# Retention attention and a feed-forward on one core: the lead-in's order of work, V scaled ahead of the masks, transposes two units ahead, all tables first

## The chip, the cores and the metric

The kernel runs on one core of one Trainium2 chip. The time is device microseconds of one execution of the whole program, loads and stores of HBM included; below, "time" is the median of several executions, and "span" the part of the one profiled execution between its first and last instruction. Engines: PE does matmuls (PEld its weight loads), DVE and ACT elementwise work, POOL (GpSimd) issues the loads, SP the stores and the DMA transposes.

## The reference

For 8 batches and 8 heads of 576 positions with head size 64, retention attention (no softmax, a decay by distance), and then a feed-forward layer on the 4608 tokens:

```python
scores = (q @ k.transpose(0, 1, 3, 2)) / sqrt(64)
gamma = 1 - 2 ** (-5 - arange(H))
ret = scores * where(rel >= 0, gamma ** rel, 0)      # rel = query position - key position
x = (ret @ v).transpose(0, 2, 1, 3).reshape(4608, 512)
h = x @ w_in                                         # 512 -> 2048
out = (h * sigmoid(1.702 * h)) @ w_out               # 2048 -> 512
```

All inputs and the output are float32 in HBM.

## The kernel before, in words

**Units and chunks.** The 4608 tokens are cut into 36 units of 128 rows; four units make a chunk of 512 tokens, so there are 9 chunks. Each pair of batches gives nine units: four of the first batch, four of the second, and one that joins the last 64 rows of both. The decay factors out as gamma^i * gamma^-j: V is scaled by gamma^-j (table `vfac`), the output by gamma^i (table `gq`), and in between only a 0/1 mask is needed. Earlier units of the same batch come in through a state, the sum of K^T V so far.

**The steps of one unit u**, by the names of the helpers:

- `transpose_pe(u, bank, eng)`: eight 128 x 128 transposes of K and Q on PE into a PSUM bank (L310), then one copy to SBUF, tile `qkT`, on ACT (L314) or DVE (L317). From unit 12 on the transposes are done by DMA from SP's queue instead (L322).
- `scores(u, 0)`: eight matmuls into banks S0 and S1 (L398); `scores_out(u, hh, 0)`: two DVE multiplies by the mask, tiles `pm_0` and `pm_1` (L407).
- `scale_v(u)`: one DVE multiply of V by `vfac`, tile `vp` (L301).
- `state_in_psum(u, "S3", eng)` or, from unit 8, `state(u, "S3")`: four matmuls of K by `vp` (L331), then copies into tile `kv` (ACT L344, DVE L346; for `state` four DVE operations from L359 on). A unit that joins two batches has none.
- `inter(u)`: matmuls of the state up to the unit before (L379, L386), none for the first unit of a batch; `values(u)`: eight matmuls of `vp` by the masked scores (L417); `values_out(u)`: one DVE multiply by `gq` into the chunk's `xT` (L427).

The feed-forward of a chunk is 16 steps `up` (four matmuls of 512 columns, L438, and a gelu on ACT, L443) and 16 steps `down` (four matmuls, L469; every fourth ends a unit: copy on ACT, L477, and store by SP, L483). Chunk 1's ups are done in halves of 256 tokens, `up_half` (L455, L460).

**The order.** Each engine works its own queue strictly in the order in which the code lists its operations; semaphore waits are derived from the tiles and PSUM banks read and written. The order of the first twelve units ("heads") is written out by hand: a lead-in with units 0 to 3, the ups of chunks 0 and 1 with units 4 to 7 between, and the downs of chunk 0 with units 8 to 11 between. `play(n, step, events)` runs n steps and calls the listed events after the step of that number. From unit 12 on (the "blocks", two units each) a loop repeats one pattern. `warm(n)` puts n matmuls of a zero tile into PE's queue (L491); their output is not used.

**Loads.** POOL issues K and Q of a unit (`load_kq`), V (`load_v`) and the weights in one queue: units 0 to 3, w_in, units 4 to 7, w_out, units 8 and on. V of units 0 and 1 alone comes over SP's queue at the very start. A load waits only until its buffer is free (12 buffers of K and Q, 10 of V).

**Tables.** `setup_first`, `setup_gq` and `setup_last` make masks and tables on DVE and ACT; `setup_last` has the parts that the joined units need. `setup_gelu` loads ACT's function table for gelu, `setup_tail` makes the joined units' mask and clears the second batch's state tiles.

Of the kernel before, what the change touches and what calls it, by code (L numbers as in the profile page):

```python
# [140 lines left out]
def bass_retnet_parallel__then__act_gelu_quick_kernel(  # L141
# [13 lines left out]
    with es:  # L155
# [40 lines left out]
        def load_kq(u):  # L196
            sl = u % NLD
            rows = unit_rows(u)
            for i, src in enumerate((k, q)):
                def f(e, src=src, i=i):  # L200
                    return [
                        e.dma_start(  # L202
                            kq[sl][p0 : p0 + n, i, :].rearrange("p (h d) -> p h d", d=DH),
                            src[b, :, s0 : s0 + n, :].rearrange("h p d -> p h d"),
                        )
                        for p0, n, b, s0 in rows
                    ]
                op("pool", f, writes=[f"kq{sl}_{i}"], dma=f"d_kq{sl}_{i}", ndma=len(rows))
# [51 lines left out]
        def setup_gq(c0, c1):  # L260
            for hp in range(HP):
                op("act", lambda e, hp=hp: e.activation(
                    gq[:, c0:c1, hp, :],
                    iota_c[:, P * c0 : P * c1].rearrange("p (c i) -> p c i", i=P),
                    AF.Exp, bias=lnsc.ap(), scale=lng[:, hp : hp + 1]),
                   reads=["iota_c", "lnsc", f"lng{hp}_0", f"lng{hp}_1"],
                   writes=[f"gq{hp}_{c}" for c in range(c0, c1)])
# [17 lines left out]
        def setup_gelu():  # L285
            op("act", lambda e: e.activation(scr.ap(), lnsc.ap(), AF.Gelu_apprx_sigmoid),
               reads=["lnsc"], writes=["scr"])
# [11 lines left out]
        def scale_v(u):  # L299
            sl, _, ty = u % NVN, *unit_info(u)[1:]  # L300
            op("dve", lambda e: e.tensor_tensor(  # L301
                vp[u % NVP].ap(), vn[sl].ap(),
                vfac[:, ty, :, None].to_broadcast([P, H, DH]), ALU.mult),
               reads=[f"vn{sl}"] + (VF if ty < 4 else VFT), writes=[f"vp{u % NVP}"])
# [65 lines left out]
        def inter(u):  # L370
            pb, kind, c = unit_info(u)
            qt = qkT[u % NQT]
            if c == 0:
                return
            bank = f"O{u % 2}"
            ob = by_pair(bank)
            for hp in range(HP):
                if kind < 2:
                    op("pe", lambda e, hp=hp: e.matmul(  # L379
                        ob[:, hp, :], kv[kind][c - 1][:, hp, :], qt[:, HP + hp, :],  # L380
                        start=(hp == 0), stop=True, skip_group_check=True),
                       reads=[f"kv{kind}_{c - 1}_0", f"kv{kind}_{c - 1}_1", f"qkT{u % NQT}"],
                       writes=[bank])
                else:
                    for b in range(2):
                        op("pe", lambda e, hp=hp, b=b: e.matmul(  # L386
                            ob[:, hp, 64 * b : 64 * b + 64], kv[b][3][:, hp, :],
                            qt[:, HP + hp, 64 * b : 64 * b + 64],
                            start=(hp == 0 and b == 0), stop=True, skip_group_check=True),
                           reads=[f"kv{b}_3_0", f"kv{b}_3_1", f"qkT{u % NQT}"], writes=[bank])  # L390

        def scores(u, sb0=None):
            sb0 = 2 * (u % 2) if sb0 is None else sb0
            qt = qkT[u % NQT]
            for hp in range(HP):
                for hh in range(2):
                    bank = f"S{sb0 + hh}"
                    op("pe", lambda e, hp=hp, hh=hh, bank=bank: e.matmul(  # L398
                        by_pair(bank)[:, hp, :], qt[64 * hh : 64 * hh + 64, hp, :],
                        qt[64 * hh : 64 * hh + 64, HP + hp, :], skip_group_check=True),  # L400
                       reads=[f"qkT{u % NQT}"], writes=[bank])

        def scores_out(u, hh, sb0=None):
            sb0 = 2 * (u % 2) if sb0 is None else sb0
            m = maskc if unit_info(u)[1] == 2 else mask
            bank = f"S{sb0 + hh}"
            op("dve", lambda e: e.tensor_tensor(  # L407
                pm[u % 4][hh].ap(), by_pair(bank), m[:, None, :].to_broadcast([P, HP, P]), ALU.mult),
               reads=[bank, "maskc" if m is maskc else "mask"], writes=[f"pm{u % 4}_{hh}"])

        def values(u):
            c = unit_info(u)[2]
            bank = f"O{u % 2}"
            ob = by_pair(bank)
            for hp in range(HP):
                for hh in range(2):
                    op("pe", lambda e, hp=hp, hh=hh: e.matmul(  # L417
                        ob[64 * hh : 64 * hh + 64, hp, :], vp[u % NVP][:, 2 * hp + hh, :],
                        pm[u % 4][hh][:, hp, :],
                        start=(c == 0 and hp == 0), stop=True, skip_group_check=True),  # L420
                       reads=[f"vp{u % NVP}", f"pm{u % 4}_{hh}"], writes=[bank])

        def values_out(u):
            ch, j = divmod(u, 4)
            ty = unit_info(u)[2]
            bank = f"O{u % 2}"
            op("dve", lambda e: e.tensor_tensor(  # L427
                xT[ch % 3][:, :, 128 * j : 128 * j + 128], by_pair(bank), gq[:, ty, :, :], ALU.mult),
               reads=[bank] + [f"gq{i}_{ty}" for i in range(HP)], writes=[f"xT{ch % 3}_{j}"])
# [58 lines left out]
        def warm(n):  # L488

            for _ in range(n):  # L490
                op("pe", lambda e: e.matmul(  # L491
                    banks["H1"].ap(), zero[:, 0:P], zero.ap(), start=True, stop=True),
                   reads=["zero"], writes=["H1"])

        def head_in(u, eng, bank="S2"):
            transpose_pe(u, bank, eng)

        def head_mid(u, eng):
            scores(u, 0)
            scores_out(u, 0, 0)  # L500
            scores_out(u, 1, 0)
            scale_v(u)
            if u < 8:
                state_in_psum(u, "S3", eng)
            else:
                state(u, "S3")

        def head_out(u):
            inter(u)
            values(u)  # L510
            values_out(u)

        def fetch(m):
            for u in (2 * m, 2 * m + 1):
# [45 lines left out]
        setup_first()  # L560
        setup_gq(0, 1)
        setup_gq(1, 4)
        load_kq(0)
        load_kq(1)
        for u in (2, 3):
# [16 lines left out]
                for f in events.get(i, ()):  # L582
                    f()

        warm(14)
        head_in(0, "dve")
        warm(3)
        head_mid(0, "act")
        warm(1)
        head_in(1, "act")  # L590
        warm(1)
        head_out(0)
        warm(1)
        head_mid(1, "act")
        warm(1)
        head_in(2, "act")
        warm(2)
        head_out(1)
        warm(1)
        head_mid(2, "act")  # L600
        setup_last()
        warm(1)
        head_in(3, "act")
        warm(2)
        head_out(2)
        warm(2)
        head_mid(3, "act")
        setup_gelu()
        setup_tail()
        warm(6)  # L610
        head_out(3)
        for u in (10, 11):
            load_kq(u)
            load_v(u)
        warm(4)
        play(16, lambda f: up(0, f), {
            10: [lambda: head_in(4, "dve")],
            12: [lambda: head_mid(4, "dve")],
            14: [lambda: head_out(4), lambda: head_in(5, "dve")],
        })  # L620
        head_mid(5, "dve")
        head_in(6, "dve")
        warm(4)
        head_out(5)
        fetch(6)
        warm(6)
        play(8, lambda i: up_half(1, i, 0), {
            0: [lambda: head_mid(6, "dve")],
            2: [lambda: head_in(7, "dve"), lambda: head_out(6)],
            4: [lambda: head_mid(7, "dve")],  # L630
            6: [lambda: head_out(7)],
        })
        fetch(7)
        play(8, lambda i: up_half(1, i, 1), {})
        play(16, lambda i: down(0, i, ("S2", "H1")), {
            2: [lambda: head_in(8, "act", "H0")],
            4: [lambda: head_mid(8, "dve")],
            6: [lambda: head_out(8), lambda: head_in(9, "act", "H0")],
            8: [lambda: head_mid(9, "dve")],
            10: [lambda: head_out(9), lambda: head_in(10, "act", "H0"), lambda: ready(6)],  # L640
            12: [lambda: head_mid(10, "dve")],
            13: [lambda: head_in(11, "act", "H0")],
            14: [lambda: head_out(10)],
            15: [lambda: head_mid(11, "dve"), lambda: fetch(8)],
        })
        play(4, lambda i: down(1, i, ("H0",)), {1: [lambda: head_out(11)]})
        for m in range(5, NU // 2 + 1):
# [74 lines left out]
```

## Time and profile before

| | |
|---|---|
| time, three executions | 344.62 us median (342.09 to 344.97) |
| the profiled execution | 346.53 us, of which span 344.7 us |
| mean granted TensorE clock in the profile | 0.965 |
| busy in the span | PE 311.8 us, DVE 131.5, ACT 127.3, POOL 106.7 |
| moved | 39.14 MB at 114 GB/s in the mean |
| first up step of chunk 0 starts at | 35.18 us |
| first down step of chunk 0 starts at | 80.25 us |
| first scores of unit 12 (blocks start) | 111.85 us |

How to read the rows of the profile: a row of the timeline has start and duration in us, engine, source line, operation, output <- inputs, shapes and the number of instructions that were merged, and in brackets how long the engine stood idle before and what released it. A row that lists stretches has the busy time of each engine with the number of instructions. A granted clock of 1.00 is full speed, 0.50 half. A row of DMA issues ends in the time from issue to landing.

### The profile page before, as it was taken

What the parts mean: (1) busy time and instruction counts of PE and PEld (TensorE: products, weight loads), DVE (VectorE), ACT (ScalarE), POOL (GpSimd) and SP (SyncE); (2) the same over time, 40 slices, a digit from 0 to 9 for tenths busy, and PEclk for the clock granted to TensorE, in tenths of its full rate; (3) what the DMA queues carried; (4) which work ended last, traced back from release to release, by engine and by line L of the source; (5) the groups of instructions that cost most, each with busy time, mean ns of one, the idle gap of its engine ahead of it and who ended that gap; (6) DMA issues with size and microseconds to landing.
All of it is one profiled execution on the core that took longest, in us unless ns stands there. A gap on an engine that the chain in (4) does not pass through costs nothing.

```text
span 344.7 us, 5147 instructions
## 1 busy us (share of the span) xinstructions
PE 311.8 (90%) x2157; PEld 161.0 (47%) x2193; DVE 131.5 (38%) x265; ACT 127.3 (37%) x226; POOL 106.7 (31%) x133
## 2 busy tenths in 40 slices
PE   7477977699777999999999999999999999999995
PEld 2343334575333454545545454545455454544442
DVE  3535046620665571705363553507262643100000
ACT  7253541244121433343433334343434333344411
POOL 9999748430525534360515160000000000000000
PEclk9855999999899999999999999999999999999999
DMA  9999999991999999998799999404040411100022
GB/s 134 194 204 178 203 191 177 178 158 28 124 136 133 154 174 154 126 155 137 96 128 155 84 176 127 91 33 91 33 91 32 95 60 25 37 30 30 32 91 61
DMA packets 114712, 39.14 MB, mean 114 GB/s; under 512 B 103809, under 2 KB 107905, under 8 KB 114689
## 3 DMA queue, kind: packets, MB, share of 16 engines
q0 software_dynamic: 82016, 22.55, 64.2%
q1 hardware_dynamic: 32672, 16.26, 26.3%
q8 instruction: 17, 0.28, 0.3%
q14 instruction: 7, 0.05, 0.1%
HBM read 36.70 MB, written 9.44 MB: 134 GB/s over the span
## 4 chain that ended last, share of the span: by engine, by line
PE 84%; DVE 6%; DMA 4%; ACT 2%; issue 2%; POOL 1%; SPq 1%; POOLq 0%; DVEq 0%
PE psS L469 30%; PE psH L438 30%; PE psH L455 4%; PE psS L398 3%; PE psO L417 3%; PE psH L469 3%; DMA qkT<-kq 3%; PE psS L331 3%; PE psH L491 2%; PE psO L469 2%; DVE pm_0 L407 2%; DVE vp L301 2%; DVE pm_1 L407 2%; PE psO L379 2%; DMA kq<-in_q_dram 1%
## 5 line engine op out<-in xcount | busy, mean ns | idle before, releaser
L438 PE MATMUL psH<-xT,w_in_sb 128*128 128x512 bf16 x498 | 125.8, 379 | 1.0 <-ACT osb L477 0.2
L443 ACT ACTIVATE gT<-psH 128x512 bf16<-128x512 f32 x128 | 76.4, 597 | 134.3 <-PE psH L438 134.3
L469 PE MATMUL psS<-w_out_sb,gT 128*128 128x512 bf16 x480 | 122.2, 383 | 2.6 <-DVE pm_0 L407 2.2
L438 PEld LDWEIGHTS psH<-xT,w_in_sb 128*128 128x128 bf16 x512 | 49.0, 98 | 60.8 <-ACT gT L443 3.5
L469 PEld LDWEIGHTS psS<-w_out_sb,gT 128*128 128x128 bf16 x496 | 46.9, 98 | 52.4 <-issue 1.6
L202 POOL DMA_DIRECT2D kq<-in_k_dram x40 | 36.8, 927 | 60.1 <-PE psS L331 57.3
L216 POOL DMA_DIRECT2D vn<-in_v_dram x38 | 35.0, 932 | 38.5 <-DVE vp L301 33.7
L202 POOL DMA_DIRECT2D kq<-in_q_dram x40 | 36.7, 926 | 0.3 <-issue 0.2
L427 DVE TENSOR_TENSOR xT<-psO,gq 128x512 bf16<-128x512 f32 x36 | 23.6, 684 | 26.2 <-PE psO L417 26.2
L331 PE MATMUL psS<-vp,kq 128*128 128x128 bf16 x128 | 13.0, 227 | 21.8 <-DVE vp L301 21.8
L407 DVE TENSOR_TENSOR pm_0<-psS,mask 128x512 bf16<-128x512 f32 x32 | 22.0, 688 | 27.5 <-PE psS L398 27.5
L361 DVE TENSOR_TENSOR kvf<-psS,kvf 64x256 f32<-64x256 f32 x24 | 10.1, 422 | 36.7 <-PE psS L331 36.5
L477 ACT ACTIVATE osb<-psS 128x512 f32<-128x512 f32 x31 | 18.5, 597 | 15.1 <-PE psS L469 15.1
L301 DVE TENSOR_TENSOR vp<-vn,vfac 128x512 bf16<-128x512 f32 x36 | 23.6, 681 | 0.0
L331 PEld LDWEIGHTS psS<-vp,kq 128*128 128x128 bf16 x128 | 9.2, 100 | 28.8 <-DVE vp L301 23.8
L407 DVE TENSOR_TENSOR pm_1<-psS,mask 128x512 bf16<-128x512 f32 x32 | 21.8, 680 | 0.0
L491 PE MATMUL psH<-zero 128*128 128x512 bf16 x46 | 17.2, 500 | 1.5 <-DVE zero L242 1.2
L460 ACT ACTIVATE gT<-psH 128x512 bf16<-128x512 f32 x16 | 9.6, 597 | 17.7 <-PE psH L455 17.7
L455 PE MATMUL psH<-xT,w_in_sb 128*128 128x256 bf16 x128 | 14.8, 273 | 0.0
L359 DVE COPY kvf<-psS 64x256 f32<-64x256 f32 x12 | 5.1, 422 | 24.5 <-PE psS L331 24.4
L398 PE MATMUL psS<-qkT 64*128 64x128 bf16 x288 | 12.9, 224 | 1.1 <-ACT qkT L314 0.7
L417 PE MATMUL psO<-pm_0,vp 128*64 128x128 bf16 x144 | 13.5, 233 | 0.0
(74 smaller groups left out, 183.3 us busy)
## 6 DMA issues: line engine op xcount, KB each, us to landing
out_dram<-osb SPq DMA_DIRECT2D x32, 256.0 KB, 2.3
vn<-in_v_dram POOLq DMA_DIRECT2D x30, 256.0 KB, 10.5
kq<-in_k_dram POOLq DMA_DIRECT2D x32, 128.0 KB, 6.3
kq<-in_q_dram POOLq DMA_DIRECT2D x32, 128.0 KB, 9.1
w_in_sb<-in_moe_w_in_dram POOLq DMA_DIRECT2D x4, 512.0 KB, 9.5
w_out_sb<-in_moe_w_out_dram POOLq DMA_DIRECT2D x4, 512.0 KB, 18.1
vn<-in_v_dram POOLq DMA_DIRECT2D x8, 128.0 KB, 7.5
out_dram<-osb SPq DMA_DIRECT2D x8, 128.0 KB, 2.4
```

The lines of the kernel that those rows point to most:

```text
L202: e.dma_start(kq[sl][p0 : p0 + n, i, :].rearrange("p (h d) -> p h d", d=DH), src[b, :, s0 : s0 + n, :].rearrange("h p d -> p h d"),)
L216: e.dma_start(vn[sl][p0 : p0 + n, :, :], v[b, :, s0 : s0 + n, :].rearrange("h p d -> p h d"),)
L301: op("dve", lambda e: e.tensor_tensor(vp[u % NVP].ap(), vn[sl].ap(), vfac[:, ty, :, None].to_broadcast([P, H, DH]), ALU.mult), reads=[f"vn ...
L331: op("pe", lambda e, hp=hp: e.matmul(kb[:, hp, :], kq[sl][:, 0, P * hp : P * hp + P], vp[u % NVP][:, 2 * hp : 2 * hp + 2, :], start=(first ...
L407: op("dve", lambda e: e.tensor_tensor(pm[u % 4][hh].ap(), by_pair(bank), m[:, None, :].to_broadcast([P, HP, P]), ALU.mult), reads=[bank, " ...
L417: op("pe", lambda e, hp=hp, hh=hh: e.matmul(ob[64 * hh : 64 * hh + 64, hp, :], vp[u % NVP][:, 2 * hp + hh, :], pm[u % 4][hh][:, hp, :], st ...
L427: op("dve", lambda e: e.tensor_tensor(xT[ch % 3][:, :, 128 * j : 128 * j + 128], by_pair(bank), gq[:, ty, :, :], ALU.mult), reads=[bank] + ...
L438: op("pe", lambda e, a=a: e.matmul(hb, w_in_sb[:, a, P * f : P * f + P], xT[c % 3][:, a, :], start=(a == 0), stop=(a == HP - 1)), reads=[f ...
L443: op("act", lambda e: e.activation(gT[c % 2][:, f, :], hb, AF.Gelu_apprx_sigmoid), reads=[bank], writes=[f"gT{c % 2}_{f}"])
L455: op("pe", lambda e, a=a, f=f, j=j: e.matmul(hb[:, j, :], w_in_sb[:, a, P * f : P * f + P], xT[c % 3][:, a, n], start=(a == 0), stop=(a == ...
L469: op("pe", lambda e, f=f: e.matmul(y, gT[c % 2][:, f, P * r : P * r + P], w_out_sb[:, f, :], start=(f == 0), stop=(f == NF - 1)), reads=[f ...
L491: op("pe", lambda e: e.matmul(banks["H1"].ap(), zero[:, 0:P], zero.ap(), start=True, stop=True), reads=["zero"], writes=["H1"])
```

## The change

- `setup_last()` is called with the other tables, ahead of everything else, instead of after unit 2's first half.
- `head_mid` is now scores, scaling of V, masks; the state moves out of it to the end of `head_out`, behind inter, values and `values_out`. The scaling of V for units 0 and 1 is listed ahead of all heads.
- The lead-in's transposes stand further ahead: unit 1's directly behind unit 0's scores, unit 2's ahead of unit 1's scores, unit 3's ahead of unit 2's. They use banks H0 and S2 in turn, where before they all used S2.
- Unit 0's `head_out` comes behind unit 1's `head_mid`, and so on. The numbers of fillers change, 49 to 30 in sum.
- Units 4 to 7 are placed earlier in the ups: unit 5 and unit 6's transposes move into chunk 0's ups.
- In the downs of chunk 0 the places of the events stay, but `head_mid` and `head_out` have their new contents.

```diff
-        def head_mid(u, eng):
+        def head_mid(u):
             scores(u, 0)
+            if u > 1:
+                scale_v(u)
             scores_out(u, 0, 0)
             scores_out(u, 1, 0)
-            scale_v(u)
+
+        def head_out(u, eng="dve"):
+            inter(u)
+            values(u)
+            values_out(u)
             if u < 8:
                 state_in_psum(u, "S3", eng)
             else:
                 state(u, "S3")
-
-        def head_out(u):
-            inter(u)
-            values(u)
-            values_out(u)
...
         setup_gq(1, 4)
+        setup_last()
...
-        warm(14)
+        scale_v(0)
+        scale_v(1)
+        warm(13)
         head_in(0, "dve")
+        warm(4)
+        head_mid(0)
+        head_in(1, "act", "H0")
         warm(3)
-        head_mid(0, "act")
+        head_in(2, "act")
+        head_mid(1)
+        head_out(0, "act")
+        head_in(3, "act", "H0")
         warm(1)
-        head_in(1, "act")
-        warm(1)
-        head_out(0)
-        warm(1)
-        head_mid(1, "act")
-        warm(1)
-        head_in(2, "act")
+        head_mid(2)
+        head_out(1, "act")
         warm(2)
-        head_out(1)
-        warm(1)
-        head_mid(2, "act")
-        setup_last()
-        warm(1)
-        head_in(3, "act")
-        warm(2)
-        head_out(2)
-        warm(2)
-        head_mid(3, "act")
+        head_mid(3)
+        head_out(2, "act")
         setup_gelu()
+        warm(4)
+        head_out(3, "act")
         setup_tail()
-        warm(6)
-        head_out(3)
...
-        warm(4)
+        warm(2)
         play(16, lambda f: up(0, f), {
-            10: [lambda: head_in(4, "dve")],
-            12: [lambda: head_mid(4, "dve")],
-            14: [lambda: head_out(4), lambda: head_in(5, "dve")],
+            9: [lambda: head_in(4, "dve")],
+            11: [lambda: head_mid(4)],
+            12: [lambda: head_in(5, "dve")],
+            13: [lambda: head_out(4)],
+            14: [lambda: head_mid(5)],
+            15: [lambda: head_in(6, "dve"), lambda: head_out(5)],
         })
-        head_mid(5, "dve")
-        head_in(6, "dve")
-        warm(4)
-        head_out(5)
         fetch(6)
-        warm(6)
+        head_mid(6)
+        head_in(7, "dve")
+        warm(1)
         play(8, lambda i: up_half(1, i, 0), {
-            0: [lambda: head_mid(6, "dve")],
-            2: [lambda: head_in(7, "dve"), lambda: head_out(6)],
-            4: [lambda: head_mid(7, "dve")],
-            6: [lambda: head_out(7)],
+            1: [lambda: head_out(6)],
+            3: [lambda: head_mid(7)],
+            5: [lambda: head_out(7)],
         })
```

More of the change, by code (lines that the diff above doesn't have):

```diff
@@ L636, in bass_retnet_parallel__then__act_gelu_quick_kernel @@
             2: [lambda: head_in(8, "act", "H0")],
-            4: [lambda: head_mid(8, "dve")],
+            4: [lambda: head_mid(8)],
             6: [lambda: head_out(8), lambda: head_in(9, "act", "H0")],
-            8: [lambda: head_mid(9, "dve")],
+            8: [lambda: head_mid(9)],
             10: [lambda: head_out(9), lambda: head_in(10, "act", "H0"), lambda: ready(6)],
-            12: [lambda: head_mid(10, "dve")],
+            12: [lambda: head_mid(10)],
             13: [lambda: head_in(11, "act", "H0")],
             14: [lambda: head_out(10)],
-            15: [lambda: head_mid(11, "dve"), lambda: fetch(8)],
+            15: [lambda: head_mid(11), lambda: fetch(8)],
         })
```

## The prediction

> **What bounds the kernel now.** I read the time by stages first. The cuts are where the first up-projection starts (35.18), where the down-projection of chunk 0 starts (80.25) and where the steady blocks start (111.85). The columns are start:end, length, busy time of PE, PEld, DVE, ACT and POOL, granted clock, DMA share and rate.
>
> ```profile
> 0.00:35.18 35.18, 24.06 (x162) 12.55 (x165) 14.66 (x41) 16.05 (x42) 34.55 (x48) 0.71 1.57 178
> 35.18:80.25 45.07, 37.00 (x324) 23.33 (x327) 16.27 (x28) 18.53 (x32) 23.06 (x28) 1.00 1.61 171
> 80.25:111.85 31.60, 25.51 (x200) 12.70 (x203) 16.65 (x30) 6.73 (x9) 12.05 (x14) 0.95 0.86 113
> 111.85:344.73 232.88, 225.25 (x1474) 112.42 (x1500) 83.90 (x166) 85.97 (x144) 37.03 (x45) 1.00 0.68 93
> ```
>
> The last stage, two thirds of the span, has PE busy for 225.25 of 232.88 us; its code is not touched, and I move it as a block. What the change can win lies ahead of 111.85. The same cut for the filler line, and the waits, say how much is loose there (waits from 35.18 to 111.85: total us, times, longest):
>
> ```profile
> 0.00:35.18 35.18, 14.90 (x37) 4.47 (x39) 0.71 1.57 178
> ```
> ```profile
> PE psS L331 <- DVE vp L301: 13.9, 7, 2.0
> ```
>
> Of 24.06 us of PE work in the lead-in, 14.90 is filler. Seven times in the next two stages, once a unit, PE stands 2.0 us at the state matmuls (L331) until V is scaled; the timeline of the lead-in has the same wait at 10.57, and shows why:
>
> ```profile
> 7.45 0.69 DVE L317 COPY qkT<-psS 128x1024 bf16<-128x1024 bf16 x1 [4.06 <-PE psS L310]
> ...
> 8.63 0.69 DVE L407 TENSOR_TENSOR pm_0<-psS,mask 128x512 bf16<-128x512 f32 x1 [0.49 <-PE psS L398]
> ...
> 9.83 0.68 DVE L301 TENSOR_TENSOR vp<-vn,vfac 128x512 bf16<-128x512 f32 x1
> ...
> 10.57 0.51 PE L331 MATMUL psS<-vp,kq 128*128 128x128 bf16 x4 [1.98 <-DVE vp L301]
> ...
> 11.12 0.77 ACT L344 ACTIVATE kv_0<-psS 64x256 bf16<-64x256 f32 x2 [4.29 <-PE psS L331]
> ...
> 12.40 1.02 ACT L314 ACTIVATE qkT<-psS 128x1024 bf16<-128x1024 bf16 x1 [0.51 <-PE psS L310]
> ...
> 13.40 0.69 DVE L427 TENSOR_TENSOR xT<-psO,gq 128x512 bf16<-128x512 f32 x1 [2.88 <-PE psO L417]
> ...
> 23.45 1.65 ACT L271 ACTIVATE gq<-iota_c,lnsc,lng 128x128 f32<-128x128 f32 x4
> ...
> 25.00 0.84 ACT L281 ACTIVATE vfac<-iota_t 128x1 f32<-128x1 f32 x8
> ```
>
> A unit is one chain: transposes, copy, scores, two mask multiplies, scaling of V, state, then the next unit's transposes behind it in PE's queue, 5 to 7 us a unit.
>
> **The change, step by step.** (1) *Tables.* The 1.65 + 0.84 us on ACT leave their place ahead of unit 3's copy. They now follow this row:
>
> ```profile
> 2.81 4.02 ACT L262 ACTIVATE gq<-iota_c,lnsc,lng 128x128 f32<-128x128 f32 x8
> ```
>
> ACT is then free at 6.83 + 2.49 = 9.3. Little is late: unit 1's transposes, the first that ACT copies, follow scores(0), which start at 8.2, by 0.35 + 0.45 and end about 9.0 (prices below); the 0.3 lie under the wait for unit 2's load. Without that cover it would cost 2.5.
>
> (2) *scale_v ahead of the masks.* It runs while PE does scores or ups, so the 2.0 us of each wait goes; the state now follows the values matmuls, which wait for the masks. What is late next is pm_1: two mask multiplies after the scores, 1.3 us by their starts 0.61 apart and 0.68 long. Units 0 and 1 are scaled as soon as V lands, before DVE has anything else. The wait added is DVE's on V's load: the masks are queued behind it, and PE's values behind them.
>
> (3) *Transposes two units ahead.* In PE's queue head_in(2) now stands ahead of scores(1), and head_in(3) ahead of scores(2): PE waits for q of unit 3 with unit 2's scores behind it. The load queue's rows, issue and landing, for q of units 3, 4 and 13, and for w_in (the median of its four):
>
> ```profile
> 8.77 0.96 POOL L202 DMA_DIRECT2D kq<-in_q_dram  x1
> ```
> ```profile
> kq<-in_q_dram POOLq DMA_DIRECT2D x1, 128.0 KB, 5.2
> ```
> ```profile
> 14.33 1.02 POOL L202 DMA_DIRECT2D kq<-in_q_dram  x1
> ```
> ```profile
> kq<-in_q_dram POOLq DMA_DIRECT2D x1, 128.0 KB, 12.7
> ```
> ```profile
> 49.29 0.87 POOL L202 DMA_DIRECT2D kq<-in_q_dram  x1 [0.25 <-issue]
> ```
> ```profile
> kq<-in_q_dram POOLq DMA_DIRECT2D x1, 128.0 KB, 14.8
> ```
>
> ```profile
> 10.52 3.07 POOL L225 DMA_DIRECT2D w_in_sb<-in_moe_w_in_dram  x4
> ```
> ```profile
> w_in_sb<-in_moe_w_in_dram POOLq DMA_DIRECT2D x4, 512.0 KB, 9.5
> ```
>
> The q land at 14.0, 27.0 and 64.1. POOL's queue is not reordered, so I keep these times. PE's prices at full clock come from the up stage, where an up step (four matmuls) follows from the starts of two gelus eight steps apart, (43.80 - 36.89) / 8 = 0.86:
>
> ```profile
> 36.89 0.60 ACT L443 ACTIVATE gT<-psH 128x512 bf16<-128x512 f32 x1 [0.27 <-PE psH L438]
> ...
> 43.80 0.60 ACT L443 ACTIVATE gT<-psH 128x512 bf16<-128x512 f32 x1 [0.27 <-PE psH L438]
> ```
> ```profile
> 51.51 0.62 PE L310 MATMUL psS<-ident,kq 128*128 128x128 bf16 x8
> ...
> 51.96 1.03 PE L438 MATMUL psH<-xT,w_in_sb 128*128 128x512 bf16 x4
> ```
> ```profile
> 56.88 0.39 PE L379 MATMUL psO<-qkT,kv_0 128*128 128x128 bf16 x4
> ...
> 57.20 0.24 PE L417 MATMUL psO<-pm_0,vp 128*64 128x128 bf16 x1
> ...
> 57.55 1.47 PE L491 MATMUL psH<-zero 128*128 128x512 bf16 x6
> ```
>
> By the distance of the starts: head_in 0.45, inter 0.32, values 0.35. Scores (eight small matmuls in pairs, like values) I take as 0.35, state (four, like inter) as 0.32 at most; a filler is a quarter of an up step, 0.22.
>
> *Lead-in.* q of unit 3 lands at 14.0, its transposes leave PE at 14.2; ACT copies until 15.4. Scores(2) 14.4 to 14.75; DVE, which has scaled V of unit 2 by then, masks until 16.1. Inter(1), values(1), state(1), two fillers: to 16.1. Scores(3) 16.2; DVE has xT of unit 1 (0.7), scale_v(3) (0.7) and the masks to do: until 18.6. PE meanwhile does head_out(2), ACT its state and the gelu table; values(3) from 18.7, xT of unit 3 behind xT of unit 2 on DVE: 19.9. So the first up starts at **20.0** instead of 35.18. The weights do not hold it: w_in is issued from 10.5 to 13.6 and takes 9.5, so to about 23, the last quarter being wanted only 12 steps after the first up, at 30.
>
> *Ups of chunks 0 and 1.* 32 steps x 0.86 = 27.6. Heads 4 to 7: 4 x (0.45 + 0.35 + 0.35 + 0.32) + 3 x 0.32 = 6.8, one filler 0.2, and the first values' wait for pm_1 in units 5 and 6, 0.5 + 0.3, as no up stands between. 35.4 us, so down starts at **55.4** instead of 80.25. q of unit 4 is asked for at 20.0 + 10 steps = 28.6 and is there at 27.0.
>
> *Down of chunk 0.* 20 steps, 17.3; heads 8 to 11, where unit 8 has no state and unit 9 no inter, 4 x (0.45 + 0.35 + 0.35) + 6 x 0.32 = 6.5; waits for pm at units 10 and 11, where DVE has just had scaling of 12 and 13 (1.3) and four state pieces (1.75): 0.5 and 1.1. 25.4, so the blocks start at **80.8** instead of 111.85. Here three of the 2.0 us waits go, and a stretch at half clock that they lead to (92.6, below; half of 3.4 us, 1.7).
>
> My placing leaves out small hops. Doing the old 35.18 to 80.25 the same way (27.6 + 6.8, ten fillers 2.2, four waits of 2.0) gives 44.6 for 45.07, the old down stage (17.3 + 6.5, three waits 6.0, clock 1.7) 31.5 for 31.60: 0.6 short together, and with the lead-in I add 1.5. The blocks start at 82.3, **29.5 earlier**. The profiled execution took 346.5 us (span 344.7 and 1.8 around it): 317.0. It lay 1.9 above the median 344.62, which would be 315.1. I say **316**.
>
> **The clock** is the unknown that the order itself sets. Windows of 3.4 us, cut where the granted clock changes:
>
> ```profile
> 7.30:10.70 3.40, 1.28 (x16) 0.50 (x14) 2.58 (x4) 0.00 (x0) 3.40 (x5) 1.00 1.92 176
> 10.70:14.10 3.40, 2.93 (x28) 2.00 (x29) 0.69 (x1) 1.78 (x3) 3.40 (x5) 0.50 1.70 181
> 14.10:17.50 3.40, 1.42 (x23) 1.01 (x18) 1.89 (x3) 0.72 (x2) 3.40 (x5) 1.00 1.24 205
> ...
> 51.70:55.10 3.40, 1.66 (x20) 0.79 (x17) 2.91 (x5) 0.76 (x2) 3.11 (x4) 1.00 1.91 176
> ...
> 89.20:92.60 3.40, 1.42 (x17) 0.71 (x16) 1.89 (x3) 0.60 (x2) 1.05 (x2) 1.00 1.19 192
> 92.60:96.00 3.40, 3.40 (x12) 0.99 (x11) 1.72 (x4) 0.00 (x0) 2.65 (x3) 0.51 1.87 160
> ```
>
> A window with 1.28 or 1.42 us of PE work is followed by one at half clock, one with 1.66 is not. In the new lead-in the thin window is 10.7 to 14.1, where PE waits for unit 3: transposes 0.4, scores 0.4, values 0.5, state 0.3, half of head_in(3): about 1.75. So I take full clock, closely.
>
> The Trainium skill, "TensorE: Matmul & The Clock Gate", Part 4, says that transposes do not count as PE activity; by it the window would hold 1.2 counted us and the clock would halve. This trace speaks rather against it: 10.7 to 14.1, with eight transposes in its 2.93 us, was followed by full clock.
>
> **The rivals.** *R1, the clock halves at 14.1.* For: the margin above, fewer fillers (30 for 49 in the code), and the windows' phase may differ in another execution. Least: one window does 3.4 us at half speed, 1.7 late: 318. Most: from 14.2 to the first up there are 5.3 us of PE work, which double, and the first 3.4 us of ups too (1.7): 7 late, 323.
>
> *R2, the loads or the transposes by DMA become late.* The early blocks take K and Q by DMA transposes. Now q of unit 13 is there at 64.1, asked for at about 68, while loads still run. The first one issued in a block, its landing, and the scores that wait for its pair (blocks' own start is 111.85):
>
> ```profile
> 113.01 4.59 SPq L322 DMA_TRANSPOSE qkT<-kq  x2
> ```
> ```profile
> qkT<-kq SPq DMA_TRANSPOSE x1, 10.5
> ```
> ```profile
> 124.47 0.40 PE L398 MATMUL psS<-qkT 64*128 64x128 bf16 x8 [0.25 <-DMA qkT<-kq]
> ```
>
> Issued at 68, a pair that takes 11.5 lands near 79.5, wanted at 82. If the crowded queues make it 15, PE stands 2; twice, and with V of unit 13 late on DVE, 4 to 8 in all: 320 to 324. Against: transposes landed in 10.5 in the middle of loads.
>
> *R3, it does not do what it says: the lead-in is bound by the load stream.* Then 14.0 moves: every us by which unit 3 lands later is a us of the first up, and unit 4 has only 1.6 in hand. Loads later by a tenth give 318; the POOL queue, unchanged, speaks against.
>
> *R4, slower.* In each block two DMA transposes must land within the 11.5 us until their scores, and the row at 124.47 shows them just late. If the loads, pulled forward against the outputs, push each pair past that in all 12 pairs, PE stands 12 times; from 2.5 us each, a pair in 14, the 30 are gone: at 2.9 it is 316 + 35 = 351. Against it: the last stage loads at 93 GB/s of the 178 seen at the start.
>
> **How the numbers follow.** The forecast 0.56 (312 to 319, both bases and the hops), R1 0.22, R2 0.13, R3 0.05, R4 0.02, and 0.02 for a start past 24 us for other reasons. Range 311 to 324: low, 315.1 without the hops (313.6) and another 2.5, by which the lowest run, 342.09, lies under the median; high, R1 whole and R2. A measurement here tells 1% from no change: faster 0.96, same 0.02, slower 0.02.
>
> **What would show it.** First up near 20 and no half clock after 4 us; no wait of L331 on vp; first down near 55; first scores by DMA-transposed K near 82, and from there 233 us as before. It is wrong if the first up starts past 24, if half clock runs into the ups, or if scores wait on qkT's DMA.

## The result, and the profile after

The changed kernel takes **325.04 us** in the median of four executions (323.71 to 328.03), the kernel before 344.8: a ratio of 0.9455, 95% interval 0.9374 to 0.9537. The direction was right; the time lies 1.0 us above the upper end of the range (311 to 324), and the gain is 19.8 us where 29 were forecast. The profiled execution took 323.71 us, span 321.9.

The profile after, cut where the same work starts as in the cut of before: first up, first down, first scores of unit 12, end.

```profile
0.00:20.04 20.04, 15.85 (x151) 7.99 (x154) 13.18 (x36) 15.23 (x41) 19.41 (x29) 1.00 1.48 169
20.04:55.99 35.95, 35.46 (x314) 23.00 (x319) 18.53 (x35) 19.22 (x34) 27.67 (x34) 1.00 1.64 190
55.99:81.37 25.38, 24.18 (x200) 12.54 (x203) 15.58 (x29) 6.74 (x9) 16.85 (x21) 1.00 1.75 158
81.37:321.90 240.53, 227.63 (x1473) 113.07 (x1500) 84.67 (x167) 85.97 (x144) 42.76 (x51) 0.99 0.87 104
```

| stage | before | forecast | after |
|---|---|---|---|
| lead-in, to the first up | 35.18 | 20.0 | 20.04 |
| ups of chunks 0 and 1 | 45.07 | 35.4 | 35.95 |
| downs of chunk 0 | 31.60 | 25.4 | 25.38 |
| blocks, to the end | 232.88 | 232.9 | 240.53 |

Three stages came within 0.6 us. The miss lies in the one whose code was not touched, 7.65 us longer than before. The waits of PE in that stage (total us, times, longest), and the two rows of the timeline at its start, unit 12's scores and unit 13's:

```profile
PE psS L398 <- DMA qkT<-kq: 6.1, 4, 3.4
PE psS L469 <- DVE pm_0 L407: 1.5, 7, 0.2
```
```profile
81.37 0.40 PE L398 MATMUL psS<-qkT 64*128 64x128 bf16 x8
85.15 0.40 PE L398 MATMUL psS<-qkT 64*128 64x128 bf16 x8 [3.38 <-DMA qkT<-kq]
```

Scores wait 6.1 us for transposes by DMA. The kernel before, in the same stage, had this row:

```profile
PE psS L398 <- DMA qkT<-kq: 0.3, 1, 0.3
```

Behind the first long wait comes a window at half clock, 3.4 us long; half of it, 1.7, is my estimate of its cost:

```profile
86.40:89.80 3.40, 3.40 (x10) 1.24 (x9) 1.67 (x3) 1.19 (x2) 1.39 (x3) 0.51 1.64 189
```

5.8 more of waiting and 1.7 make 7.5 of the 7.65. The chain that ended last points to the same place by its shares; before, the DMA transposes had 3% of it, now 14%:

```profile
PE psS L469 28%; PE psH L438 27%; DMA qkT<-kq 14%; PE psH L455 4%; PE psO L417 3%; PE psO L469 2%; PE psS L398 2%; POOL kq L202 2%; PE psS L331 2%; SPq L322 2%; PE psH L469 2%; DMA kq<-in_q_dram 2%; PE psO L379 1%; DVE vp L301 1%; ACT osb L477 1%
```

The first pair's transposes, their issue on SP's queue and the times to landing of the one and the other:

```profile
66.04 7.24 SPq L322 DMA_TRANSPOSE qkT<-kq  x2
```
```profile
qkT<-kq SPq DMA_TRANSPOSE x1, 15.0
```
```profile
qkT<-kq SPq DMA_TRANSPOSE x1, 17.4
```

In the kernel before this pair took 6.8 and 7.9 (issue and first landing):

```profile
90.30 4.06 SPq L322 DMA_TRANSPOSE qkT<-kq  x2
```
```profile
qkT<-kq SPq DMA_TRANSPOSE x1, 6.8
```

### The profile page after: what moved, and what is told of

It reads as the page before. It is cut to its first block, busy times and chain, and to the rows that moved or that the text cites. A ratio compares the mean times of both kernels' runs of the same rounds, so it can differ in the third digit from the quotient of the medians.

```text
span 321.9 us, 5110 instructions
## 1 busy us (share of the span) xinstructions
PE 303.1 (94%) x2137; PEld 156.6 (49%) x2174; DVE 132.0 (41%) x265; ACT 127.2 (40%) x226; POOL 106.7 (33%) x133
## 4 chain that ended last, share of the span: by engine, by line
PE 72%; DMA 16%; DVE 4%; POOL 2%; SPq 2%; issue 1%; ACT 1%; POOLq 0%
PE psS L469 28%; PE psH L438 27%; DMA qkT<-kq 14%; PE psH L455 4%; PE psO L417 3%; PE psO L469 2%; PE psS L398 2%; POOL kq L202 2%; PE psS L331 2%; SPq L322 2%; PE psH L469 2%; DMA kq<-in_q_dram 2%; PE psO L379 1%; DVE vp L301 1%; ACT osb L477 1%
## 5 line engine op out<-in xcount | busy, mean ns | idle before, releaser
L438 PE MATMUL psH<-xT,w_in_sb 128*128 128x512 bf16 x498 | 128.0, 383 | 0.8
L469 PE MATMUL psS<-w_out_sb,gT 128*128 128x512 bf16 x479 | 120.6, 379 | 2.3 <-DVE pm_0 L407 1.5
L216 POOL DMA_DIRECT2D vn<-in_v_dram x38 | 35.0, 934 | 11.5 <-DVE pm_0 L407 5.7
L361 DVE TENSOR_TENSOR kvf<-psS,kvf 64x256 f32<-64x256 f32 x24 | 10.1, 421 | 35.7 <-PE psS L331 35.5
L398 PEld LDWEIGHTS psS<-qkT 64*128 64x128 bf16 x288 | 8.2, 94 | 12.3 <-DMA qkT<-kq 4.0
L367 DVE TENSOR_TENSOR kv_3<-psS,kvf 64x256 bf16<-64x256 f32 x12 | 5.1, 422 | 21.7 <-PE psS L331 21.6
L417 PE MATMUL psO<-pm_0,vp 128*64 128x128 bf16 x144 | 13.3, 224 | 0.2 <-DVE pm_0 L407 0.2
L417 PE MATMUL psO<-pm_1,vp 128*64 128x128 bf16 x144 | 12.5, 223 | 1.0 <-DVE pm_1 L407 1.0
```

The source lines that it names most:

```text
L216: e.dma_start(vn[sl][p0 : p0 + n, :, :], v[b, :, s0 : s0 + n, :].rearrange("h p d -> p h d"),)
L398: op("pe", lambda e, hp=hp, hh=hh, bank=bank: e.matmul(by_pair(bank)[:, hp, :], qt[64 * hh : 64 * hh + 64, hp, :], qt[64 * hh : 64 * hh + ...
L417: op("pe", lambda e, hp=hp, hh=hh: e.matmul(ob[64 * hh : 64 * hh + 64, hp, :], vp[u % NVP][:, 2 * hp + hh, :], pm[u % 4][hh][:, hp, :], st ...
L438: op("pe", lambda e, a=a: e.matmul(hb, w_in_sb[:, a, P * f : P * f + P], xT[c % 3][:, a, :], start=(a == 0), stop=(a == HP - 1)), reads=[f ...
L469: op("pe", lambda e, f=f: e.matmul(y, gT[c % 2][:, f, P * r : P * r + P], w_out_sb[:, f, :], start=(f == 0), stop=(f == NF - 1)), reads=[f ...
```

## The experiments

Theory A: a transpose by DMA loses time because it meets loads that are still running. Theory B: it is slow at this place for its own reasons. Theory C: the blocks are slower for another reason. All times are medians beside runs of the kernel before (343 to 345 us in each comparison).

**The yardstick**, the changed kernel again.

> The changed kernel once more, as the yardstick of its neighbours: about 325 us. In its first profile the first up-projection step starts at 20.0, the first down step at 56.0, the scores of unit 12 at 81.4, and the scores of unit 13 wait 3.4 us for a transpose by DMA; all theories expect the same again.

Measured: 327.21 (325.27 to 328.73), ratio 0.9502 [0.9437, 0.9567]. First up 20.35, first down 56.08, scores of unit 12 at 81.07, the wait for unit 13 5.0 us. The row of its blocks and of its waits:

```profile
81.07:326.90 245.83, 231.84 (x1501) 113.46 (x1500) 84.64 (x167) 85.98 (x144) 41.96 (x51) 0.99 0.94 102
```
```profile
PE psS L398 <- DMA qkT<-kq: 9.9, 5, 5.0
```

So the three early stages repeat within 0.4, and the blocks do not: they are 12.95 us longer than before here, 7.65 in the other execution. Between these two profiled executions, the fastest and the slowest of eight (323.71 and 328.73), the blocks differ by 5.3 us: 3.8 more of waiting for transposes, and two windows at half clock about the first wait instead of one, with 5.77 us of PE work for 3.40, an estimated 1.2.

**Units 12 and 13 transposed on PE.**

```diff
-            10: [..., lambda: ready(6)],
+            10: [..., lambda: scale_v(12), lambda: scale_v(13)],
...
-            13: [lambda: head_in(11, "act", "H0")],
-            14: [lambda: head_out(10)],
+            13: [lambda: head_in(11, "act", "H0"), lambda: head_in(12, "act", "S2")],
+            14: [lambda: head_out(10), lambda: head_in(13, "act", "H0")],
```

> Units 12 and 13 are transposed on TensorE (banks S2 and H0, copies on ACT) instead of by DMA. Theory A (the transposes by DMA lose time because they share the DMA engines with loads that are still running): the 3.4 us wait goes, the half clock after it (1.7 us) goes, TensorE pays 0.9; the loads behind, no longer interleaved with this pair, finish sooner, so the next pairs (issued from about 83) take about 10 us as in the kernel before: 317 to 319. Theory B (a transpose by DMA is slow at this place of SP's queue by itself, for its stores and its own descriptors): the first wait goes too, but the later pairs keep their 15 to 17 us and their waits of 2.7 us in sum: 320 to 322. Theory C (the loss after 81 is not the transposes but the rest of the blocks, slower for another reason): 324 or more.

Measured: 325.34 (324.48 to 328.71), ratio 0.9469 [0.9400, 0.9539]. The first wait is gone, and the next pair has it:

```profile
101.50 0.61 PE L398 MATMUL psS<-qkT 64*128 64x128 bf16 x8 [4.80 <-DMA qkT<-kq]
```

The number that theory A was given here was wrong: the loads behind did not get out of the way of the next pairs. By itself the run speaks for B or C as much as for A; its time lies in the range given for C.

**Loads that wait for the transposes.** The loads of each pair of units from 14 on wait until the pair before has been transposed:

```diff
+        def gate(u):
+            p = u - u % 2 - 2
+            return [f"qkT{x % NQT}" for x in (p, p + 1)] if u >= 14 else []
...
-                op("pool", f, writes=[f"kq{sl}_{i}"], ...)
+                op("pool", f, reads=gate(u), writes=[f"kq{sl}_{i}"], ...)
...
-            op(eng, f, writes=[f"vn{sl}"], ...)
+            op(eng, f, reads=gate(u), writes=[f"vn{sl}"], ...)
...
-            fetch(m + 4)
-            ready(m + 2)
+            ready(m + 2)
+            fetch(m + 3)
```

In the code of the heads `fetch(7)` moves behind `ready(6)`, and `fetch(8)` goes, since block 5 now does it.

> The loads of each pair of units from 14 on wait until the DMA transposes of the pair before have landed, so that loads and transposes no longer run at the same time; nothing else moves. Theory A: each transpose lands within 8 us of its issue, scores never wait for one, 316 to 318, unless a load comes too late for its use (a wait of DVE on V or of SP on K and Q would show it). Theory B: the transposes keep 15 to 17 us, their scores wait as before, 323 or more, later still as the loads are held back.

Measured: **316.45** (315.35 to 317.39), ratio 0.9187 [0.9130, 0.9244]. The same rows as above, of this kernel: issue and landing of the first pair, PE's longest stage and the first one.

```profile
67.50 2.76 SPq L326 DMA_TRANSPOSE qkT<-kq  x2
```
```profile
qkT<-kq SPq DMA_TRANSPOSE x1, 3.4
```
```profile
0.00:21.55 21.55, 18.47 (x154) 9.30 (x154) 13.28 (x36) 15.24 (x41) 20.92 (x31) 0.92 1.43 171
...
82.64:315.10 232.46, 228.33 (x1501) 112.33 (x1500) 85.37 (x167) 85.98 (x144) 57.61 (x69) 1.00 0.72 107
```

The first pair, which took 15 and 17 us, lands after 3.4 and 3.1; the median of all 24 transposes is 3.4 and the longest, which met loads of V, 8.7. No scores wait for one; the blocks take 232.46, as before (232.88). Holding the loads back made the kernel 9 to 11 us faster (316.45 against 325.04 and 327.21). This is theory A, and against B and C.

**The same collision made in the kernel before.** Its loads from unit 14 on are held back, so that they run when its first pair is transposed:

```diff
-                    load_kq(u)
+                    load_kq(u, ["osb0"] if u == 14 else [])      # POOL waits for the first output tile
...
-        fetch(7)
...
-            4: [lambda: head_mid(8, "dve")],
+            4: [lambda: head_mid(8, "dve"), lambda: fetch(7)],
```

> The kernel before, with its loads from unit 14 on held back until the first output tile of chunk 0 has been made (about 84 us), so that they run while the first transposes by DMA are issued (90.3). There the pair landed 6.8 and 7.9 us after issue. Theory A: now 12 us or more each, and the block's start may wait for them (2 to 5 us slower). Theory B: 7 to 8 us as before, and the same time.

Measured: 355.71 (two executions, 354.25 and 357.17), ratio 1.0333 [1.0242, 1.0424]. The blocks, cut at unit 12's scores:

```profile
112.40:352.40 240.00, 230.41 (x1501) 113.30 (x1500) 83.91 (x166) 85.99 (x144) 37.02 (x45) 0.99 0.77 97
```

The lead-in is the old one (first up 35.52), the blocks are 7.1 us longer than before. The first pair took 8.3 and 13.9 us, the next 13.9 and 15.3: later than A's 12 for all but the first. The collision needs only loads that are still running, not the change. Of the 7.1, scores wait 5.4 us for transposes (0.3 before), and behind that wait two windows ran at half clock.

**The gate on the kernel before**, alone.

> The kernel before, with the same gate on the loads and nothing else: how much of the gated kernel's gain is the gate by itself. Theory A: before, scores waited 0.3 us for a transpose in all, so the gate has little to give: 342 to 346. If the gate were a gain of its own, whatever the lead-in: 336.

Measured: 344.6 (342.47 to 345.31, ten executions), ratio 1.0003 [0.9962, 1.0043]. The gate is worth nothing in a kernel whose scores hardly wait for transposes, though some of its pairs did meet loads; the 9 to 11 us that it gives back in the changed kernel are that kernel's own.

**Only K and Q gated.** The gate taken off `load_v`.

> The kernel with gated loads, but only K's and Q's loads (128-byte packets) wait for the transposes, V's (4 KB packets) do not and run when their buffers are free. If any load beside a transpose slows it: transposes of 6 to 12 us, 318 to 322. If it is the small packets alone: transposes of 3 to 4 us as gated, 316 to 317.

Measured: 315.75 (315.66 to 317.11), ratio 0.9197 [0.9120, 0.9274]. Inconclusive: V's loads wait for their buffers anyway, and met hardly more transposes than in the gated kernel. The pair of units 16 and 17, counted from its first packet to its last, met about 60 packets of V in both kernels and took 6.3 us there and 6.7 here, against 2.9 undisturbed. The next pair met 16 there and 51 here and took 3.0 and 3.6. Some packets of K and Q were among them (30 and 78 beside the first pair, 0 and 55 beside the next), so that V's packets alone slow a transpose is likely and not shown.

The rest ask which part made the lead-in 15 us shorter. They stand on the gated kernel (316.45), whose blocks are steady, and undo one part each.

**Tables late**: `setup_last()` behind `head_mid(2)`.

> The kernel with gated loads, and the late tables (setup_last) back behind unit 2's first half. By the prediction's step 1 (2.5 us of ACT, hidden only while the loads are waited for), ACT makes them from 15.4 to 17.9, state(1)'s copy and inter(2) come about 2.1 later, and the first up starts 2 later: 318 to 319 against 316.5 for the gated kernel. A rival that ACT has room anyway: no change.

Measured: 317.81 (317.05 to 318.73), ratio 0.9243 [0.9176, 0.9311]; first up 23.40. In the lead-in PE now stands 1.7 us for ACT's copy of a state (L348 in this kernel), a wait that the gated kernel does not have.

**Masks first**: `scale_v(u)` behind the two `scores_out` in `head_mid`.

> The kernel with gated loads, and the scaling of V back behind the two mask multiplies in head_mid (the state stays behind values). By the prediction's step 2: 0.8 later at the first up, and in units 5 to 7, 10 and 11 the values, which wait for the scaled V too, come up to 0.7 later each: 318 to 320. Rival: the win was in moving the state behind the values, not in the place of the scaling, and the downs hide the rest: within 1 us of 316.5.

Measured: 317.21 (315.64 to 317.82), ratio 0.9218 [0.9148, 0.9288]; first up 22.82. The time lies within 1 us of the gated kernel's, which is the rival's case. This profile has 6.8 us of half clock in the lead-in, the gated kernel's 3.4, so the 1.3 at the first up may be the clock.

**Transposes one ahead**: `head_in(2)` behind `head_out(0)`, `head_in(3)` behind `head_out(1)`.

> The kernel with gated loads; in the lead-in the transposes of units 2 and 3 stand one unit ahead (behind head_out(0) and head_out(1)) instead of two; the fillers keep their number less none. If the lead-in hangs on the landing of unit 3's q (14.0), as the prediction's timetable has it, the order of the transposes costs nothing, at most 1 us: 316 to 317.5, first up within 1 of the gated kernel's. If two ahead is what shortened the lead-in: first up 2 to 4 later, 318 to 320.

Measured: 315.93 (315.82 to 316.27), ratio 0.9190 [0.9114, 0.9267]; first up 20.51.

**Fillers out**: of the lead-in's 29 fillers ahead of the first up the first 13 kept.

> The kernel with gated loads, and of the lead-in's fillers only the first 13 kept (16 taken out). By the prediction's rival R1 the clock halves in the lead-in and stays so into the ups: first up 2 to 5 later, ups at half clock for 3.4 us or more, 319 to 324. If the fillers do nothing for the clock: 316.

Measured: 319.05 (316.33 to 319.75), ratio 0.9264 [0.9186, 0.9341]; in the profiled execution, one of 316.33, the first up at 20.54 and one window at half clock. That execution, with a mean granted clock of 0.995, is not the usual one: the other three had 0.976 to 0.978 and took 318.88 to 319.75. So the 16 fillers are worth about 3 us in most executions, by the clock, as R1 has it at its low end.

**The old order of units**: `head_out(u)` ahead of `head_mid(u + 1)`, transposes one ahead.

```diff
-        head_in(2, "act")
-        head_mid(1)
         head_out(0, "act")
-        head_in(3, "act", "H0")
+        head_mid(1)
+        head_in(2, "act")
         warm(1)
-        head_mid(2)
         head_out(1, "act")
+        head_mid(2)
+        head_in(3, "act", "H0")
...
```

> The kernel with gated loads, and in the lead-in the old order of units: head_out(u) ahead of head_mid(u+1), transposes one unit ahead; the scaling ahead of the masks, the state behind the values, the tables and the number of fillers as in the changed kernel. If the interleaving of units is what shortened the lead-in: first up 3 or more later than 20 to 21.5, 319 or more. If it is not (unit 3's chain from its q at 14.0 sets the end either way, as the one-ahead run has it): first up at 19 to 21, 315 to 317.

Measured: **315.24** (314.55 to 315.48), ratio 0.9172 [0.9108, 0.9235]; first up 19.76.

**The kernel before, gated, without its fillers** (the first 14 kept).

> The kernel before with gated loads (344.6), and of the fillers ahead of the first ups only the first 14 kept. If the old lead-in was long because of its fillers, which ran at half clock and stood on the chain (about 6 us of them), the first up starts 4 to 6 earlier, 339 to 341. If they were in waits that another engine sets anyway, within 2 us of 344.6, or slower by ups at half clock.

Measured: 342.51 to 348.39 us in four executions (three of them at 348.3 to 348.4), no gain that can be told. In the profile, one of the three, the first up came at 31.47, 2.2 earlier than in the gated kernel before (33.62), and the scores of unit 12 at 114.04, 3.5 later (110.52): with most fillers gone the clock stood at half from 10.1 to 34.0, past the first up, and for three more windows in the ups. So taking them out gives 2 us of the old lead-in and loses more behind it; what they would cost at an unchanged clock is not shown.

**The state back ahead of the transposes**, in the old order of units, lead-in only; and then **the scaling back behind the masks as well** (units 0 and 1 no longer scaled ahead), which is the old chain:

```diff
         def head_mid(u):
             scores(u, 0)
-            if u > 1:
+            if u > 3:                       # second kernel only
                 scale_v(u)
             scores_out(u, 0, 0)
             scores_out(u, 1, 0)
+            if u < 4:
+                scale_v(u)                  # second kernel only
+                state_mid(u, "act")         # both: the state matmuls and copies, no longer in head_out
```

> The kernel with gated loads and the old unit order (315.2; first up 19.8), and in the lead-in the state matmuls back into head_mid, ahead of the next unit's transposes; the scaling stays ahead of the masks. If the state's place alone stretches the chain: first up 3 or more later. If it hurts only while it waits for the scaled V: V is there by then, first up within 1 of 19.8, 315 to 316.5.

Measured: 315.74 (315.71 to 315.81), ratio 0.9187 [0.9103, 0.9270]; first up 20.43.

> As before, and in the lead-in the scaling of V back behind the masks: the old chain of scores, masks, scaling, state, transposes of the next unit, with the new tables and few fillers. If this chain is what made the old lead-in long (5.2 us from state to state, four units): first up at 26 to 29, 322 or more. If not: 20 to 22, 315 to 318.

Measured: 325.92 (325.47 to 326.86), ratio 0.9487 [0.9413, 0.9560]; first up 29.37. The state matmuls of units 1 to 3 in its timeline:

```profile
15.35 0.40 PE L335 MATMUL psS<-vp,kq 128*128 128x128 bf16 x4 [1.98 <-DVE vp L305]
...
20.01 0.40 PE L335 MATMUL psS<-vp,kq 128*128 128x128 bf16 x4 [1.98 <-DVE vp L305]
...
25.27 0.61 PE L335 MATMUL psS<-vp,kq 128*128 128x128 bf16 x4 [2.04 <-DVE vp L305]
```

From state to state 4.7 to 5.3 us again. PE waits at the state matmuls for the scaled V four times in this lead-in, 8.0 us in all (the kernel before: four times, 7.9); with the state back alone it is 1.1, with the masks first alone nothing. Neither place alone costs over 1.3 us at the first up (masks first; state back 0.7), both together 9.6, and 10.7 in the time, against the old-order kernel: the 2.0 us wait comes only when the state stands ahead of the transposes and its V is scaled last. Taking either away is enough. Two limits: the run with the masks first alone has the new order of units and scales units 0 and 1 ahead, so the two halves were not undone on one and the same kernel; and from 20.7 us on this lead-in ran at half clock (granted 0.50), with 6.41 us of PE work, so up to 3.2 of the 9.6 may be the clock.

With the old chain the first up is at 29.37; the kernel before had it at 35.18. Of the 5.8 us between, the late tables are about 1.9; the rest, which may be its ten more fillers and its longer time at half clock, no run separates.

## Why the prediction was right in part, and where it failed

**Right: the chain, and the timetable built on it.** The lead-in, the ups and the downs came within 0.04, 0.55 and 0.02 us. The lead-in's timetable held step by step, not only at its end: unit 3's scores start at 16.08 (16.2 forecast), its values at 18.84 (18.7), and the first up at 20.04 (20.0). The 2.0 us waits at L331 are gone. The hops that were added (1.5) were not needed: unit 12's scores came at 81.37, not 82.3.

**Right in sum, not in the parts.** The timetable had unit 3's q at 14.0 as the lead-in's end in any order, and the one-ahead and old-order kernels bear it out: step 3 (transposes two ahead, units interleaved) is worth nothing here, 315.93 and 315.24 for 316.45. Step 1's 2.5 us "without that cover" measured 1.4 in the time (317.81), 1.9 at the first up, each of the two profiles having one window at half clock. Step 2 carries the lead-in, but as one half of a pair: the waits that it was to remove come back, 8.0 us in all, only when the state is in its old place too.

**R1 happened, at about its least price.** The clock halved in the lead-in in some executions. The gated kernel's profile is one:

```profile
10.60:14.00 3.40, 1.80 (x28) 1.16 (x29) 2.23 (x4) 1.80 (x4) 3.40 (x6) 1.00 1.72 176
14.00:17.40 3.40, 3.40 (x30) 2.08 (x31) 2.05 (x4) 1.17 (x2) 3.40 (x5) 0.50 1.23 200
```

Its first up is at 21.55 against 20.04 to 20.5 in the profiles without it: 1.1 to 1.5 for R1's 1.7. But the reading under it, that 1.42 us of PE work in a window halves the clock and 1.66 does not, fell: here 1.80 halved it, and in the gated kernel without the later fillers 2.33 did:

```profile
15.10:18.60 3.50, 2.33 (x38) 1.47 (x32) 3.50 (x7) 1.99 (x6) 3.50 (x5) 1.00 1.23 206
18.60:22.00 3.40, 2.75 (x19) 1.47 (x18) 2.73 (x8) 1.96 (x4) 3.40 (x5) 0.50 1.25 205
```

So the busy time of PE in a window does not decide by itself. Nor do the transposes explain it, which by the Trainium skill ("TensorE: Matmul & The Clock Gate", Part 4) do not count as busy in the same way: the window of 2.33 us holds none. The prediction's argument against that page does not hold either. Without its transposes the window from 10.7 to 14.1 still has 2.28 us of PE work, more than the 1.66 that the prediction took to be enough, so full clock behind it tells nothing of them. What decides stays open.

**Wrong: "its code is not touched, and I move it as a block".** Code that was not touched met loads that had not moved: POOL's queue is as fast as before, the heads are 30 us faster, and so the first pairs are transposed among loads that were mostly done before: beside the first pair ran 2857 packets of K and Q loads, in the kernel before 518. The sign of it was in the text as R2, with the mechanism, the place and a price of 4 to 8 us; 7.65 came in one execution and 12.95 in another. The term that was mis-sized is the landing of a pair among loads: 11.5 us taken, 15 as the bad case, 15.0 and 17.4 measured. The 11.5 came from a row of before that was itself half disturbed, and "transposes landed in 10.5 in the middle of loads" was read as a price when it was a symptom: undisturbed they land in 3.4. With that seen, R2 would have been the likeliest case and not 0.13, and the forecast 316 + 7 to 13. Without the collision the sum holds, the gated kernel taking 316.45, but with some luck: in its profile the scores of unit 12 come at 82.64 for the 82.3 forecast because a window at half clock, which the forecast left out, stands in place of the hops that did not come.

**The base.** The 316 lies between two bases, the profiled execution of before (346.5) and the median (344.62). Of the changed kernel the profiled execution was the fastest of four (323.71 for 325.04); this adds 1.3 to the miss.

**R3 and R4** did not happen. R4's mechanism is the one that came, in its early blocks alone; in the kernel before with late loads it does end on the slower side, by 12 us.

## What to carry to other kernels

When a stage ahead gets faster, ask which queue does not, and what the untouched code will meet there: take a transfer's time alone and its time in a crowd as two prices, and look in the trace for both before moving a stage "as a block". A wait can need two conditions at once, so undo parts in pairs too: here two places cost about 1 us each alone and 10.7 together. And loads that run as far ahead as buffers allow are not free; holding them until the transposes are through was worth 9 to 11 us here, and nothing in the kernel before, where scores waited only 0.3 us for a transpose.

## What the runs showed of the hardware

A DMA transpose and loads that run at the same time slow each other, by more than an even sharing would. Counted from the trace's packets, by kind, with the mean time of one packet:

```
                                     256 B (transposes)   128 B (K, Q loads)
gated kernel, 70 to 72 us            1100 x  21 ns           0
changed kernel, 68 to 70 us             0                 1183 x 32 ns
changed kernel, 74 to 76 us           328 x  95 ns         309 x 63 ns
changed kernel, 76 to 78 us           344 x 105 ns         348 x 57 ns
```

From 74 to 78 the two kinds make 332 packets a us together, where loads alone make 592 and transposes alone at least 550 (the pair ends at 71.65); taking turns evenly would give a rate between these two. The means hide how the time is lost. Most packets of either kind take 31 ns in the crowd (the median from 74 to 80), and some stand for 0.2 to 1.5 us, several at once, ending together. What holds them up the trace does not tell.

The pair's 2048 packets take 2.9 us alone and 12.0 here, and the first of them starts 5.1 us after the issue, alone 1.3. The rate (last column, GB/s) of the two stretches, the changed kernel's first, then the gated one's:

```profile
74.00:80.00 6.00, 5.10 (x49) 2.83 (x51) 4.85 (x10) 0.60 (x1) 0.89 (x1) 1.00 1.69 70
```
```profile
68.00:72.00 4.00, 4.00 (x35) 2.02 (x32) 2.99 (x8) 1.50 (x2) 0.00 (x0) 1.00 0.86 186
```

The packets' times add up to 1.69 times the time of the DMA engines there, and the two kinds move 70 GB/s together, where either kind alone moves more than twice that (186 in the second row, transposes and a store; 196 in the changed kernel from 68 to 70, loads alone but for a few packets of a store, half of the bytes in V's 4 KB packets). Of the pairs that can be told apart in eight of these profiles, the kernel before among them, those that met more than 400 of the small packets took 4.4 to 13 us, and those that met no load 2.8 to 4.2. A store ran beside nearly all of the latter, the short ones too.
